# The end of a fill stage between attention and a feed-forward block: a second place for its x, earlier splits, stores reordered on the queue

## Chip, core, metric

One Trainium2 chip, one core. The metric is device time in microseconds (us) of one execution, from the first instruction to the last and the little around them. Engines: PE (TensorE: matmuls and their weight loads), DVE (VectorE), ACT (ScalarE), POOL (GpSimd), and SP, which here only issues transfers; ACT issues some too. Each engine works through its own list of instructions in order.

## The reference, cut

```
q_p, k_p = phi(q), phi(k)    # phi: x @ w_phi, minus max |.| of the row, then exp of it and of its negative
kv  = einsum('bhsf,bhsd->bhfd', k_p, v);  z = k_p.sum(axis=2)
num = einsum('bhsf,bhfd->bhsd', q_p, kv)
den = einsum('bhsf,bhf->bhs', q_p, z)[..., None] + 1e-06
x   = (num / den).transpose(0, 2, 1, 3).reshape(4608, 512)      # 8 batches of 576 tokens, 8 heads of 64
rms = sqrt(mean(x * x, axis=-1, keepdims=True) + 1e-06)
xn  = x / rms * rms_g
g, val = xn @ w_gate, xn @ w_val                                # 512 -> 1536
out = (g * sigmoid(g) * val) @ w_out                            # 1536 -> 512
```
All float32.

## The kernel before

**Attention.** 32 pairs (8 batches of 4 pairs of heads) run through a software pipeline: in loop turn i the front of pair i, the middle of pair i-1, the numerators of pair i-2 and the division of pair i-3 are interleaved. A matmul operand in float32 is written as a high part (a rounded copy, by ACT) and a low part (the difference), and a product is three matmuls: high by high, low by high, high by low. The helper `_split` (lines 60 and 61) makes such a pair.

**The division.** In `back`, a pair's denominators go to memory (`dd`, line 444), come back spread over partitions (`dr`, 448), are inverted on DVE (450), go out (`di`, 451) and come back broadcast (`rc`, 453; one buffer). `last` multiplies the numerators by them (467 and 468, DVE) and stores the result to `xs` (471 to 474, SP). These steps of one pair follow one another through memory.

**The fill.** The first three of the twelve 128-wide column blocks of both input weights (`fg`, `fv`) are ready during attention, and their products fill PE's gaps: 18 blocks of 256 tokens, b0 to b17. `fetch` (150, issued by ACT) loads a block's x, `fill` splits it (`xoh` by ACT, then `xol` by DVE), `squares` prepares the sum of squares (two ACT instructions, 157, and two POOL additions, 158 and 160), and six units follow, each of 12 matmuls (502): three column blocks by two weights. After two units one ACT copy (`fo`, 507) empties the PSUM bank, and a transfer that ACT issues stores it (508). `total` (165) sums the squares by four small matmuls, and a small ACT copy (`sums`, 167) takes the result. Some seven blocks are done with the last pairs; the rest follows in a loop at the end (699 to 716), together with the preparation of the remaining weights: `combine_u` (636) forms sums of quarters for a Strassen-like product in `stg` and splits them into `wh` and `wl` (DVE and POOL). `late()` puts instructions behind the last ones given to ACT, DVE and POOL so far.

**Places for x.** A block's x lies in the large buffer `xip` (even blocks) or in a side buffer (odd blocks). From loop turn 27 on the large one holds `x0`, the first 512 tokens for the next stage, and every block goes to the side buffer, one at a time: `load_x` then keeps one block in flight, and its transfer waits until the former block's `xol` has been read out of the buffer.

**Then** comes the feed-forward block over 9 blocks of 512 tokens (matmuls at line 772, evictions 780 to 800), and last the output product (line 1016). Both are untouched but for the buffer of `operands_x` (`sq`, `ss`). Tiles get their buffers from pools, and a scheduler with a cost model fixes the order in which each engine's list stands.

Of the kernel before, what the change touches and what calls it, by code (L numbers as in the profile page):

```python
# [82 lines left out]
def kernel(ctx: ExitStack, tc: tile.TileContext, q, k, v, w_phi,  # L83
# [60 lines left out]

    held = []

    def fetch(bk, n=T, queue=None):
        side = len(xips) > 1 and n == TF and (held or bk % 2)
        x = xips[-1 if side else 0].tile([128, NC * (TF if side else T)], F32, name="x")[:, 0:NC * n].rearrange("p (c t) -> p c t", c=NC)
        (queue or nc.sync).dma_start(out=x, in_=xsv[:, :, bk * n:(bk + 1) * n])  # L150
        return x

    def squares(x):
        ss = xm.tile([128, T], F32, name="ss", bufs=1)
        sq = xm.tile([128, T], F32, name="sq", bufs=1)
        for d, c in ((ss, 0), (sq, 2)):
            nc.scalar.activation(d.rearrange("p (c t) -> p c t", c=2), x[:, c:c + 2], AF.Square)
        nc.gpsimd.tensor_tensor(ss, ss, sq, ALU.add)
        s2 = xmf.tile([128, TF], F32, name="sl", bufs=2)
        nc.gpsimd.tensor_tensor(s2, ss[:, 0:TF], ss[:, TF:T], ALU.add)  # L160
        return s2
# [30 lines left out]

    waiting = set()

    @contextmanager
# [229 lines left out]
    def back(pr):  # L425
# [21 lines left out]
        def inv():  # L447
            nc.sync.dma_start(out=dr, in_=dd.rearrange("h (p x) -> (h p) x", p=64))
            with late():
                nc.vector.reciprocal(dr, dr)  # L450
            nc.sync.dma_start(out=di.rearrange("h (p x) -> (h p) x", p=64), in_=dr)
            rc = ndp.tile([64, 2, S], F32, name="rc", bufs=1)
            nc.sync.dma_start(out=rc, in_=di.unsqueeze(0).broadcast_to([64, 2, S]))
            d.update(nd=nd, rc=rc)

        return [(0.05, lambda: num(0, 0)), (0.2, lambda: num(0, 1)), (0.35, lambda: num(1, 0)),
                (0.5, lambda: num(1, 1)), (0.79, inv)]


    def last(pr):  # L460
        d = st.pop(pr)
        nd, rc, b, hp = d["nd"], d["rc"], d["b"], d["hp"]

        def fin():
            xt = nd[0]
            with late():
                nc.vector.tensor_tensor(xt[0:64], nd[0][0:64], rc[:, 0], ALU.mult)
                nc.vector.tensor_tensor(xt[64:128], nd[1][0:64], rc[:, 1], ALU.mult)
            r0, c0 = hp * 128, b * S
            if b % 2 == 0:  # L470
                nc.sync.dma_start(out=xs[r0:r0 + 128, c0:c0 + S], in_=xt)
            else:
                nc.sync.dma_start(out=xs[r0:r0 + 128, c0:c0 + SR], in_=xt[:, SM:S])
                nc.sync.dma_start(out=xs[r0:r0 + 128, c0 + SR:c0 + S], in_=xt[:, 0:SM])
            if hp == NP - 1:
                while blocks and blocks[0] * TF + TF <= (b + 1) * S:
                    fills.append(blocks.pop(0))

        return [(0.65 if pr < PR - 3 else 1.2, fin)]
# [5 lines left out]
    def fill(bk, xr):  # L485
        xx = dict(zip("hl", (xfp.tile([128, NC, TF], F32R, name="xo" + n) for n in "hl")))
        with late():
            _split(nc, xx["h"], xx["l"], xr)
        with late():
            s2 = squares(xr)  # L490
        o = {}

        def unit(j, wi):
# [11 lines left out]
            if wi:  # L505
                r = xfp.tile([128, 2, TF], F32, name="fo", bufs=3)
                nc.scalar.copy(r, fp)  # L507
                (nc.scalar if tail else nc.sync).dma_start(out=gvv[j][:, :, bk * TF:(bk + 1) * TF], in_=r)
# [20 lines left out]
    def load_x():  # L529
        while fills and len(here) < (1 if held else 2):  # L530
            bk = fills.pop(0)
            here.append((bk, fetch(bk, TF, nc.scalar)))

# [14 lines left out]
    for i in range(PR + 3):  # L548
# [20 lines left out]
        if i <= PR and len(units) + (len(fills) + len(here)) * J1 * 2 > RES:  # L569
# [4 lines left out]
            _merge([now])  # L574
        if i == PR - 5:
            x0 = fetch(0)
            held.append(x0)
        if not PR - 5 <= i < PR - 3:
            load_x()
        if i + 2 < PR:  # L580
# [55 lines left out]
    def combine_u(u):  # L636
# [7 lines left out]
        ve(t[:, 3], a12, t[:, 1], ALU.subtract)  # L644
        for src, o0, o1, eng in ((w[:, 0:2], OA11, OA22, nc.vector), (w[:, 3:4], OA22, OS1, nc.vector), (t, OS1, 7, nc.gpsimd)):
            for (hi, at_), (lo, _) in zip(places(u, o0, o1, 0), places(u, o0, o1, 1)):
                _split(nc, hi, lo, src[:, at_], lo_eng=eng)

    def operands_x(x, scratch=None):
# [4 lines left out]
        b11, b12, b21, b22 = X(0, 0), X(0, 1), X(1, 0), X(1, 1)  # L654
        t1, t2 = scratch or (xm.tile([128, T], F32, name=n, bufs=1).rearrange("p (c n) -> p c n", c=2) for n in ("sq", "ss"))
        po = nc.gpsimd.tensor_tensor
# [38 lines left out]
    with late():  # L695
        invert_new(1)
        ri = fetch_ri(0)
        norm(x0, ri)
    while units or here or fills:
        if len(units) <= 6:  # L700
            landed()
        now, units[:] = units[:6], units[6:]
        _merge([now])
        load_x()
        if len(preps) > 3:
            preps.pop(0)()
        left_ = len(units) + J1 * 2 * (len(here) + len(fills))
        if todo is None and left_ <= 18:
            with late():
                xb, todo = operands_x(x0, [stg[1][:, i * T:(i + 1) * T].rearrange("p (c n) -> p c n", c=2) for i in range(2)])  # L710
        with late():
# [377 lines left out]
```

## Time and profile before

| | |
|---|---|
| device time, 3 runs | 1277.21, 1280.15, 1286.79 us; median 1280.15 |
| the profiled execution | 1281.23 us, its span 1279.4 us |
| busy PE / DVE / ACT / POOL | 1231.3 / 958.4 / 743.1 / 701.3 us |
| mean granted clock of PE | 0.995 |
| attention, fill's end, feed-forward, output | to 488, 488 to 602, to 1014, to the end (us of the span) |

The profiled execution is 1.08 us above the median, and 1.83 us of it lie outside the span. Granted clock 1.00 is 2.4 GHz, and a window of 5 us with 0.66 holds some time at the other level, 1.2 GHz.

### The profile page before, as it was taken

What the parts mean: (1) busy time and instruction counts of PE and PEld (TensorE: products, weight loads), DVE (VectorE), ACT (ScalarE), POOL (GpSimd) and SP (SyncE); (2) the same over time, 40 slices, a digit from 0 to 9 for tenths busy, and PEclk for the clock granted to TensorE, in tenths of its full rate; (3) what the DMA queues carried; (4) which work ended last, traced back from release to release, by engine and by line L of the source; (5) the groups of instructions that cost most, each with busy time, mean ns of one, the idle gap of its engine ahead of it and who ended that gap; (6) DMA issues with size and microseconds to landing.
All of it is one profiled execution on the core that took longest, in us unless ns stands there. A gap on an engine that the chain in (4) does not pass through costs nothing. (4 is left out here: it accounts for less than half of the span.)

```text
span 1279.4 us, 27397 instructions
## 1 busy us (share of the span) xinstructions
PE 1231.3 (96%) x10401; PEld 1214.1 (95%) x10401; DVE 958.4 (75%) x1405; ACT 743.1 (58%) x1541; POOL 701.3 (55%) x649
## 2 busy tenths in 40 slices
PE   7989999999999999899999999999999899999998
PEld 7989999999999998899999999999999799999998
DVE  6998988988788653553758877877776788777785
ACT  6987897878778784564544445444434533344342
POOL 4766664667566553347435345543422067787776
PEclk9999999999999999999999999999999999999999
DMA  5555666666566425564445545556665643554443
GB/s 162 134 145 140 170 166 178 166 185 162 169 168 178 116 71 171 182 191 155 154 154 177 188 142 198 178 173 212 228 204 172 231 144 117 153 166 132 132 149 100
DMA packets 196977, 208.37 MB, mean 163 GB/s; under 512 B 67722, under 2 KB 148270, under 8 KB 196846
## 3 DMA queue, kind: packets, MB, share of 16 engines
q1 hardware_dynamic: 175982, 186.17, 48.2%
q10 hardware_dynamic: 20864, 20.45, 5.2%
q8 instruction: 82, 1.34, 0.4%
q14 instruction: 49, 0.40, 0.1%
HBM read 133.91 MB, written 72.67 MB: 161 GB/s over the span
## 5 line engine op out<-in xcount | busy, mean ns | idle before, releaser
L772 PE MATMUL r<-xo,wh 128*128 128x256 f32 x1764 | 309.9, 279 | 3.2 <-ACT c L783 1.4
L772 PEld LDWEIGHTS r<-xo,wh 128*128 128x128 f32 x1764 | 266.5, 188 | 4.7 <-ACT c L783 1.6
L405 POOL TENSOR_TENSOR ql<-eq,qh 128x256 fp32r<-128x256 f32 x256 | 215.5, 872 | 62.3 <-ACT qh L401 39.8
L772 PE MATMUL r<-xo,wl 128*128 128x256 f32 x882 | 240.9, 279 | 0.0
L772 PEld LDWEIGHTS r<-xo,wl 128*128 128x128 f32 x882 | 164.5, 188 | 0.0
L340 DVE TENSOR_REDUCE mx<-pp 128x4 f32<-128x512 f32 (+1 forms) x160 | 100.1, 631 | 48.4 <-PE pp L338 47.2
L376 PE MATMUL acc<-vm,ek 128*128 128x65 f32 x1024 | 129.9, 269 | 0.0
L376 PEld LDWEIGHTS acc<-vm,ek 128*128 128x128 f32 x1024 | 126.4, 192 | 0.1
L401 ACT ACTIVATE qh<-sm 128x512 fp32r<-128x512 f32 (+1 forms) x192 | 97.5, 508 | 0.0
L400 ACT ACTIVATE eq<-sm 128x512 f32<-128x512 f32 x128 | 78.7, 615 | 22.3 <-PE sm L389 20.7
L336 PE MATMUL pp<-wh,th 128*128 128x256 f32 x288 | 88.1, 307 | 2.7 <-DVE yk L343 1.2
L338 PE MATMUL pp<-wh,tl 128*128 128x256 f32 x288 | 84.5, 299 | 0.3 <-DVE tl L61 0.3
L502 PE MATMUL fp<-xoh,fg 128*128 128x256 f32 x344 | 73.9, 293 | 8.1 <-ACT fo L507 6.0
L337 PE MATMUL pp<-wl,th 128*128 128x256 f32 x288 | 81.7, 285 | 0.0
L61 POOL TENSOR_TENSOR xo<-x,xo 128x512 fp32r<-128x512 f32 x45 | 63.2, 1409 | 29.4 <-ACT xo L60 29.3
L363 ACT ACTIVATE ek<-yk 128x512 f32<-128x512 f32 x128 | 75.5, 656 | 2.9 <-DVE yk L343 2.6
L793 ACT ACTIVATE c<-c 128x1024 f32<-128x1024 f32 (+1 forms) x45 | 43.9, 976 | 52.6 <-DVE c L792 52.6
L502 PE MATMUL fp<-xoh,fv 128*128 128x256 f32 x344 | 72.1, 287 | 0.0
L407 POOL TENSOR_TENSOR ql<-eqr,qh 128x256 fp32r<-128x256 f32 x32 | 24.5, 765 | 84.6 <-ACT qh L401 84.6
L61 POOL TENSOR_TENSOR s2l<-st,s2h 128x768 fp32r<-128x768 f32 x17 | 39.8, 2340 | 56.1 <-ACT s2h L60 48.4
L54 POOL TENSOR_TENSOR stg<-stg,stg 128x128 f32<-128x128 f32 x48 | 24.5, 533 | 79.5 <-ACT c L789 36.4
L502 PEld LDWEIGHTS fp<-xoh,fg 128*128 128x128 f32 x344 | 57.9, 195 | 9.1 <-ACT fo L507 8.1
(263 smaller groups left out, 4166.6 us busy)
## 6 DMA issues: line engine op xcount, KB each, us to landing
ht<-hs SPq DMA_DIRECT2D x17, 1536.0 KB
hs<-c SPq DMA_DIRECT2D x36, 512.0 KB
gvr<-gvs SPq DMA_DIRECT2D x27, 512.0 KB
rc<-di SPq DMA_DIRECT2D x32, 288.0 KB
x<-xs ACTq DMA_DIRECT2D x18, 512.0 KB
x<-xs SPq DMA_DIRECT2D x9, 1024.0 KB
gvs<-fo ACTq DMA_DIRECT2D x35, 256.0 KB
kt<-in_k_dram SPq DMA_DIRECT2D x32, 256.0 KB
```

The costliest lines, as they stand in the source:

```text
L61: (lo_eng or nc.vector).tensor_tensor(lo, x, hi.bitcast(F32), ALU.subtract)
L336: nc.tensor.matmul(o, th[:, cs], wh, start=True, stop=False)
L337: nc.tensor.matmul(o, th[:, cs], wl, start=False, stop=False)
L338: nc.tensor.matmul(o, tl[:, cs], wh, start=False, stop=True)
L340: nc.vector.tensor_reduce(mx[:, 0:2 * m], pp[:, 0:2 * m], axis=AX.X, op=ALU.max, apply_absolute_value=True)
L363: nc.scalar.activation(e[h][:, sg], y["k", h], AF.Exp, scale=1.0 - 2.0 * sg)
L376: nc.tensor.matmul(acc[:, sg, h], e[h][:, sg, j], vm[:, h, j], start=False, stop=(h == 1 and j == T0 - 1))
L400: nc.scalar.activation(ei[:, sg], yi, AF.Exp, scale=1.0 - 2.0 * sg)
L401: nc.scalar.activation(hi[:, sg], yi, AF.Exp, scale=1.0 - 2.0 * sg)
L405: nc.gpsimd.tensor_tensor(lo[:, sg, cs], ei[:, sg, cs], hi[:, sg, cs].bitcast(F32), ALU.subtract)
L502: nc.tensor.matmul(fp[:, wi], w, xx[x][:, c], start=(wi == 0 and i == 0), stop=(i == 3 * NC - 1), skip_group_check=True)
L772: nc.tensor.matmul(self.r[r][:, k], w[:, cs], x[:, h, c], start=(first and k == 0 and i == 0), stop=(i == 3 * NP1 - 1), skip_group_check=True)
```

## The change

Seven edits. `fetch` gives an even block that finds the large buffer taken a second place, the tile `xo6` of the feed-forward stage's operands (empty until then). `x0` is loaded after the last block in the large buffer has been read, and multiplied by the norm (`norm`) with its operands. `load_x` keeps two blocks in flight. The loop at the end splits a block after the units of the one two places ahead, and the squares are one ACT instruction of 1024 columns behind ACT's latest. The middle eviction of a block is DVE's after attention. The lower parts of `t` in `combine_u` go from POOL to DVE. The stores of the last four pairs stand behind the latest `rc` load.

```
+            x = spare[0].tile([128, 2, 2, TF], F32R, name="xo6").bitcast(F32).rearrange("p a b t -> p (a b) t")
-        for d, c in ((ss, 0), (sq, 2)):
-            nc.scalar.activation(d.rearrange("p (c t) -> p c t", c=2), x[:, c:c + 2], AF.Square)
+        nc.scalar.activation(sq.rearrange("p (c t) -> p c t", c=NC), x, AF.Square)
...
+            loaded.append(latest(mybir.EngineType.SP))
...
+            with tc.issue_after(loaded[-1]) if pr >= PR - NP else nullcontext():
...
-        with late():
+        with tc.issue_after(latest(mybir.EngineType.Activation)):
             s2 = squares(xr)
...
-                nc.scalar.copy(r, fp)
+                (nc.vector.tensor_copy if ended and j == 1 else nc.scalar.copy)(r, fp)
...
-        while fills and len(here) < (1 if held else 2):
+        while fills and len(here) < 2:
...
-        if i == PR - 5:
-            x0 = fetch(0)
-            held.append(x0)
-        if not PR - 5 <= i < PR - 3:
-            load_x()
+        load_x()
...
-        for src, o0, o1, eng in ((w[:, 0:2], OA11, OA22, nc.vector), (w[:, 3:4], OA22, OS1, nc.vector), (t, OS1, 7, nc.gpsimd)):
+        for src, o0, o1, eng in ((w[:, 0:2], OA11, OA22, nc.vector), (w[:, 3:4], OA22, OS1, nc.vector), (t, OS1, 7, nc.vector)):
...
-        norm(x0, ri)
+    x0, held = None, [bk for bk, _ in here if bk % 2 == 0]
+    spare.append(xops[0])
+    if len(units) <= 6:
+        landed()
     while units or here or fills:
-        if len(units) <= 6:
-            landed()
+        if x0 is None and not any(bk in held for bk, _ in here):
+            x0 = fetch(0)
         now, units[:] = units[:6], units[6:]
         _merge([now])
+        landed()
         load_x()
...
             with late():
+                norm(x0, ri)
                 xb, todo = operands_x(x0, [stg[1][:, i * T:(i + 1) * T].rearrange("p (c n) -> p c n", c=2) for i in range(2)])
```

The order of the other instructions shifts as well, from about the first fill block on (the first difference on ACT is its squares, at 93 us of the span before), since the scheduler places them anew. The counts of PE's and SP's instructions stay the same; DVE has 20 more, POOL 11 and ACT 27 fewer.

SP's queue, at the denominators of the last two pairs, from the `rc` load of the last but one; before:

```order
L453 DMA rc<-di 64x1152
L444 DMA dd<-nd 1x576
L473 DMA xs<-nd 128x64
L474 DMA xs<-nd 128x512
L633 DMA stg_8088<-wgvs 128x1024
L444 DMA dd<-nd 1x576
L633 DMA wx<-wgvs 128x1024
L448 DMA dr<-dd 128x9
L451 DMA di<-dr 128x9
L453 DMA rc<-di 64x1152
```

and after:

```order
L458 DMA rc<-di 64x1152
L482 DMA xs<-nd 128x64
L483 DMA xs<-nd 128x512
L449 DMA dd<-nd 1x576
L639 DMA stg_8068<-wgvs 128x1024
L639 DMA wx<-wgvs 128x1024
L449 DMA dd<-nd 1x576
L453 DMA dr<-dd 128x9
L456 DMA di<-dr 128x9
L458 DMA rc<-di 64x1152
L482 DMA xs<-nd 128x64
L483 DMA xs<-nd 128x512
```

What moved are the stores of the last but one pair, which stood ahead of the last pair's second `dd` and now stand behind its `rc` (the stores at the top of the second list are those of the pair before it), and the weight load into `wx`, now ahead of that `dd`.

ACT's list for one block in the loop at the end (`L150`/`L153` is the load of a later block's x); before:

```order
L507 COPY fo<-fp 128x512
L167 COPY sums<-sm 128x2
L508 DMA gvs<-fo 128x2x256
L150 DMA x<-xs 128x4x256
L60 CAST wh_8072<-wx 128x512
L60 CAST wh_8072<-wx 128x256
L60 CAST wh_8072<-stg_8089 128x1024
L507 COPY fo<-fp 128x512
L157 ACTIVATE ss<-x 128x512
L157 ACTIVATE sq<-x 128x512
L508 DMA gvs<-fo 128x2x256
L507 COPY fo<-sm 128x512
```

and after:

```order
L516 COPY fo<-fp 128x512
L169 COPY sums<-sm 128x2
L60 CAST xoh<-xo_8196 128x1024
L158 ACTIVATE sq<-xo_8196 128x1024
L517 DMA gvs<-fo 128x2x256
L153 DMA xo_8308<-xs 128x4x256
L60 CAST wh_8052<-wx 128x512
L60 CAST wh_8052<-wx 128x256
L60 CAST wh_8052<-stg_8069 128x1024
L517 DMA gvs<-fo 128x2x256
L516 COPY fo<-sm 128x512
```

The split and the squares of a block now stand right behind an eviction and ahead of the next load; before, the load stood between them, and the `fo` copy that is missing now is DVE's.

DVE's list at the start of the feed-forward block (`L747`/`L761` and later evict it; `fg`, `wx` belong to the last weights); before:

```order
L641 TENSOR_TENSOR stg_8089<-stg_8088 128x256
L642 TENSOR_TENSOR stg_8089<-stg_8088 128x256
L61 TENSOR_TENSOR fg_86<-stg_8088,fg_85 128x512
L61 TENSOR_TENSOR fg_86<-stg_8088,fg_85 128x256
L747 TENSOR_TENSOR gvr<-gvr,ri 128x1024
L800 TENSOR_TENSOR c_9116<-c_9116,c_9117 128x2x256
L643 TENSOR_TENSOR stg_8089<-stg_8089,stg_8088 128x256
L749 TENSOR_TENSOR gvr<-gvr 128x512
L799 TENSOR_TENSOR c_9116<-c_9116,r_9118 128x2x256
L644 TENSOR_TENSOR stg_8089<-stg_8088,stg_8089 128x256
```

and after:

```order
L61 TENSOR_TENSOR fg_86<-stg_8068,fg_85 128x512
L61 TENSOR_TENSOR fg_86<-stg_8068,fg_85 128x256
L761 TENSOR_TENSOR gvr<-gvr,ri 128x1024
L814 TENSOR_TENSOR c_9080<-c_9080,c_9081 128x2x256
L649 TENSOR_TENSOR stg_8069<-stg_8069,stg_8068 128x256
L763 TENSOR_TENSOR gvr<-gvr 128x512
L813 TENSOR_TENSOR c_9080<-c_9080,r_9082 128x2x256
L650 TENSOR_TENSOR stg_8069<-stg_8068,stg_8069 128x256
L806 TENSOR_TENSOR c_9187<-c_9187,r_9203 128x2x256
L61 TENSOR_TENSOR fg_86<-stg_8069,fg_85 128x768
L810 TENSOR_TENSOR c_9188<-c_9188,r_9189 128x512
L61 TENSOR_TENSOR wx<-stg_8069,wx 128x256
```

The lower parts of 128x768 (`fg`) and 128x256 (`wx`) are new here, and once more for `fv`; they were POOL's.

## Rows read from the trace of the kernel before

**Rows 1.** Windows by stage: from:to, length, busy us of each engine, granted clock, DMA, GB/s.
```profile
107.00:480.00 373.00, 364.75 (x3071) 358.88 (x3071) 302.45 (x525) 302.53 (x737) 230.35 (x288) 1.00 0.57 155
487.84:601.90 114.06, 104.82 (x866) 103.00 (x865) 51.52 (x63) 56.41 (x104) 53.53 (x39) 0.97 0.57 176
487.84:521.00 33.16, 27.30 (x216) 26.65 (x215) 8.22 (x12) 10.70 (x21) 5.61 (x6) 0.95 0.59 182
521.00:601.90 80.90, 77.53 (x653) 76.35 (x652) 43.30 (x52) 45.70 (x84) 47.92 (x33) 0.98 0.56 173
615.00:642.00 27.00, 25.59 (x217) 25.19 (x217) 26.29 (x36) 12.78 (x22) 15.09 (x9) 1.00 0.44 149
```

**Rows 2.** The same columns for the fill's matmuls (line 502) alone.
```profile
487.84:601.90 114.06, 101.13 (x816) 98.03 (x816) 0.97 0.57 176
515.00:520.00 5.00, 4.33 (x25) 4.03 (x24) 0.66 0.59 203
566.00:571.00 5.00, 4.18 (x22) 4.18 (x23) 0.66 0.54 192
```

**Rows 3.** Timeline: start, length, engine, line, tiles; PE from 531.64 to 537.45.
```profile
531.64 0.28 PE L502 MATMUL sm<-xoh,fg 128*128 128x256 f32 x1
...
534.36 0.28 PE L502 MATMUL fp<-xoh,fg 128*128 128x256 f32 x1
...
536.97 0.28 PE L502 MATMUL fp<-xoh,fv 128*128 128x256 f32 x1
...
537.45 0.36 PE L502 MATMUL fp<-xoh,fg 128*128 128x256 f32 x1
```

**Rows 4.** Waits of PE from 487.84 to 604: us, times, longest.
```profile
PE fp L502 <- ACT fo L507: 6.0, 3, 3.5
PE fp L502 <- ACT sums L167: 1.8, 3, 0.8
```

**Rows 5.** Timeline of ACT and its queue; in brackets idle before, and its releaser.
```profile
513.65 0.37 ACTq L150 DMA_DIRECT2D x<-xs  x1
514.11 0.59 ACT L507 COPY fo<-fp 128x512 f32<-128x512 f32 x1 [6.54 <-DVE xol L61]
...
533.08 0.93 ACT L60 CAST wh<-wx 128x512 fp32r<-128x512 f32 x2 [3.16 <-DVE xol L61]
```

**Rows 6.** Timeline of DVE, 493 to 538.
```profile
493.42 1.41 DVE L467 TENSOR_TENSOR nd<-nd,rc 64x576 f32<-64x576 f32 x1 [7.03 <-DMA rc<-di]
...
505.10 0.21 DVE L450 RECIPROCAL dr<-dr 128x9 f32<-128x9 f32 x1 [2.50 <-DMA dr<-dd]
...
510.79 0.75 DVE L467 TENSOR_TENSOR nd<-nd,rc 64x576 f32<-64x576 f32 x1 [5.20 <-DMA rc<-di]
...
512.33 1.23 DVE L61 TENSOR_TENSOR xol<-x,xoh 128x1024 fp32r<-128x1024 f32 x1
...
533.07 4.92 DVE L187 SCALAR_TENSOR_TENSOR x<-x,g,ri 128x512 f32<-128x512 f32 x4 [0.43 <-DMA ri<-rid]
```

**Rows 7.** Timeline of SP's queue, 496 to 507: when each transfer is issued.
```profile
496.06 0.32 SPq L473 DMA_DIRECT2D xs<-nd  x1
...
496.91 0.42 SPq L633 DMA_DIRECT2D stg<-wgvs  x1
497.43 0.26 SPq L444 DMA_DIRECT2D dd<-nd  x1
...
507.07 0.46 SPq L453 DMA_DIRECT2D rc<-di  x1
```

**Rows 8.** Groups of 487 to 604: busy us, mean ns | idle before, releaser.
```profile
L61 POOL TENSOR_TENSOR wl<-stg,wh 128x1024 fp32r<-128x1024 f32 x6 | 14.3, 2390 | 24.8 <-ACT wh L60 24.8
...
L61 DVE TENSOR_TENSOR xol<-x,xoh 128x1024 fp32r<-128x1024 f32 x10 | 14.0, 1402 | 12.3 <-ACT xoh L60 12.2
```

**Rows 9.** Waits of PE from 600 to 700.
```profile
PE r L772 <- DVE c L799: 1.4, 2, 1.2
```

**Rows 10.** A window inside the attention stage; columns as in the first group.
```profile
280.00:285.00 5.00, 4.44 (x24) 4.44 (x25) 1.77 (x4) 1.60 (x5) 2.93 (x4) 0.66 0.90 270
```

More of the change, by code (lines that the diff above doesn't have):

```diff
@@ L1 @@
-from contextlib import ExitStack, contextmanager
+from contextlib import ExitStack, contextmanager, nullcontext
 import concourse.bass as bass
@@ L143 @@
     sums = gl.tile([128, N // 128], F32, name="sums")
-    held = []
+    spare = []
     def fetch(bk, n=T, queue=None):
-        side = len(xips) > 1 and n == TF and (held or bk % 2)
-        x = xips[-1 if side else 0].tile([128, NC * (TF if side else T)], F32, name="x")[:, 0:NC * n].rearrange("p (c t) -> p c t", c=NC)
+        if n == TF and spare and bk % 2 == 0:
+            x = spare[0].tile([128, 2, 2, TF], F32R, name="xo6").bitcast(F32).rearrange("p a b t -> p (a b) t")
+        else:
+            side = n == TF and bk % 2
+            x = xips[-1 if side else 0].tile([128, NC * (TF if side else T)], F32, name="x")[:, 0:NC * n].rearrange("p (c t) -> p c t", c=NC)
         (queue or nc.sync).dma_start(out=x, in_=xsv[:, :, bk * n:(bk + 1) * n])
@@ L153, in squares @@
     def squares(x):
-        ss = xm.tile([128, T], F32, name="ss", bufs=1)
-        sq = xm.tile([128, T], F32, name="sq", bufs=1)
-        for d, c in ((ss, 0), (sq, 2)):
-            nc.scalar.activation(d.rearrange("p (c t) -> p c t", c=2), x[:, c:c + 2], AF.Square)
-        nc.gpsimd.tensor_tensor(ss, ss, sq, ALU.add)
+        sq = xm.tile([128, 2 * T], F32, name="sq", bufs=1)
+        nc.scalar.activation(sq.rearrange("p (c t) -> p c t", c=NC), x, AF.Square)
+        ss = sq[:, 0:T]
+        nc.gpsimd.tensor_tensor(ss, ss, sq[:, T:2 * T], ALU.add)
         s2 = xmf.tile([128, TF], F32, name="sl", bufs=2)
@@ L193, with latest @@
     waiting = set()
+    def latest(eng):
+        return next(i for i in reversed(nc.cur_bb.bb.instructions[-300:]) if i.engine == eng)
     @contextmanager
@@ L454, in inv @@
             d.update(nd=nd, rc=rc)
+            loaded.append(latest(mybir.EngineType.SP))
         return [(0.05, lambda: num(0, 0)), (0.2, lambda: num(0, 1)), (0.35, lambda: num(1, 0)),
                 (0.5, lambda: num(1, 1)), (0.79, inv)]
+    loaded = []
     def last(pr):
@@ L469, in fin @@
             r0, c0 = hp * 128, b * S
[L470 to L474, printed above, removed]
+            with tc.issue_after(loaded[-1]) if pr >= PR - NP else nullcontext():
+                if b % 2 == 0:
+                    nc.sync.dma_start(out=xs[r0:r0 + 128, c0:c0 + S], in_=xt)
+                else:
+                    nc.sync.dma_start(out=xs[r0:r0 + 128, c0:c0 + SR], in_=xt[:, SM:S])
+                    nc.sync.dma_start(out=xs[r0:r0 + 128, c0 + SR:c0 + S], in_=xt[:, 0:SM])
             if hp == NP - 1:
@@ L529, in load_x @@
     def load_x():
-        while fills and len(here) < (1 if held else 2):
+        while fills and len(here) < 2:
             bk = fills.pop(0)
-            here.append((bk, fetch(bk, TF, nc.scalar)))
+            with tc.issue_after(latest(mybir.EngineType.Activation)) if tail else nullcontext():
+                here.append((bk, fetch(bk, TF, nc.scalar)))
     def landed():
@@ L654, in operands_x @@
         b11, b12, b21, b22 = X(0, 0), X(0, 1), X(1, 0), X(1, 1)
-        t1, t2 = scratch or (xm.tile([128, T], F32, name=n, bufs=1).rearrange("p (c n) -> p c n", c=2) for n in ("sq", "ss"))
+        if not scratch:
+            sq = xm.tile([128, 2 * T], F32, name="sq", bufs=1)
+            scratch = [sq[:, i * T:(i + 1) * T].rearrange("p (c n) -> p c n", c=2) for i in range(2)]
+        t1, t2 = scratch
         po = nc.gpsimd.tensor_tensor
```

## The prediction

> **What bounds the kernel now.** I read the windows by stage first. Over the whole run TensorE is busy 1231.3 of 1279.4 us, so only its idle time and its time at the lower clock can be won. Most of what this change touches lies between the last numerators (487.84) and the first matmul of the feed-forward block (601.90): 114.06 us, of which PE is busy 104.82, so idle 9.24, at a mean granted clock of 0.97 [rows 1]. The split at 521.00 shows where: 5.86 of the idle time is in the first 33.16 us, 3.37 in the other 80.90 [rows 1].
>
> Then the fill's matmuls alone. The stage holds 816 of them [rows 2]: 24 left over and 11 blocks of 72. When nothing disturbs them, 24 take from 531.64 to 534.36, 0.1133 us each; where the sums stand between two of them, the step is 0.48 (536.97 to 537.45), 0.37 more [rows 3]. So the stage can't be shorter than 816 x 0.1133 + 11 x 0.37 = 92.5 + 4.1 = 96.6 us, and its **excess is 17.5 us**. Of that, 9.24 is idle. Two windows of 5 us show clock 0.66, that is, time at 1.2 GHz right behind idle stretches: 25 and 22 matmuls in 4.33 and 4.18 us of busy time [rows 2], which at 0.1133 would take 2.83 and 2.49, so 1.5 and 1.7 us are lost to the clock. Idle time and clock together make 12.4 us: 7.4 in the first part and 5.1 in the second. The other 5.1 no row of mine names.
>
> Next the waits: PE's largest in the stage is for the PSUM bank that ACT's `fo` copy must empty, 6.0 us in three waits, the longest 3.5; ACT's `sums` copy adds 1.8 [rows 4]. Last, what ACT did then. At 513.65 its queue issues the load of the next block's x, and the `fo` copy behind it starts at 514.11 after 6.54 us idle, released by DVE's `xol` [rows 5]: the load may not start before `xol` has read the one place, and the copy stands behind the load in ACT's list. That `xol` ran at 512.33, behind the multiplications of the last pair, which began at 510.79 after 5.20 us of waiting for `rc` [rows 6]. And `rc` was late because SP's queue held the last pair's second `dd` until 497.43, behind the stores of pair 30 (496.06), which wait for multiplications that themselves began at 493.42 after a wait of 7.03 for their own `rc` [rows 6, 7]. In the later blocks the same pattern is smaller: at 533.08 ACT starts a copy after 3.16 us, released by `xol` [rows 5].
>
> **The change part by part.** *Stores behind `rc`.* The last `dd` no longer waits for multiplications of pair 30. From `dd` to `rc` took 497.43 to 510.79, 13.4 us [rows 6, 7]; issued at about 490, after the numerators end at 487.84 and are evicted, it lets the last multiplications start near 503, some 7 us earlier. What is queued behind the moved stores: the loads of the last blocks' x, which need the last pair's rows in memory. They wait for the last multiplications anyway, and these come earlier; I cost the move at nothing there. The chain has a new neighbour: `stg` and `wx`, the weight loads, now stand ahead of that `dd` on SP. Each issue takes about 0.4 us [rows 7], so 0.8 us if they can start at once.
>
> *Two places, split two blocks ahead.* The load of a later block then waits for an `xol` that lies a block back, and stands behind a split that is done early. The 6.0 us of `fo` waits lose their cause. What is late next is the `xol` of the second block, behind the last multiplications on DVE: 503 + 1.5 + 1.23 = 505.7 [rows 6]. The block in work at that time began at about 497.3, when its `xol` ended (493.42 + 1.41 + 1.2 + 1.23) [rows 6], and lasts 72 x 0.1133 + 0.37 = 8.5, until 505.8. So it is just in time; I leave 1.4 of the first part's 7.4 us, and **gain 6**. In the second part ACT has a copy and an instruction of squares fewer in each block, and its load waits for nothing that is late; I leave 1.1 of 5.1 and **gain 4**. Of the 5.1 us without a name I take **2**, since what follows an idle stretch goes with it. Together 12; the bounds are 0 (every wait finds a successor) and 17.5 (the whole excess).
>
> *Copies and lower parts to DVE.* In the stage, DVE is busy 43.30 of 80.90 us in the second part [rows 1]. POOL's lower parts of 128x1024 took 2390 ns each, six of them; on DVE the nearest row is `xol` of the same shape, 1402 ns [rows 8]: six cost 8.4 us there. Nine `fo` copies of 512 columns at the 0.59 of ACT [rows 5] are 5.3 more: 57 of 81, hidden beside PE as long as the order doesn't put a copy behind a wait. Taken at zero here; if that cover is gone it is the rival below. The multiplication of `x0` by the norm, 4.92 us in four instructions at 533 [rows 6], now comes some four blocks later, ahead of the operands of the first feed-forward group. By the order those are the last work of the stage on POOL and DVE, so the bounds are 0 and 3 us (most of the multiplication), and I take **1**, nearer to zero since the block it falls in has slack of about 2.5 (8.5 less 57/81 of it).
>
> *The start of the feed-forward block.* From 615 to 642 DVE is busy 26.29 of 27.00 us, PE 25.59 [rows 1], and PE already waits there for DVE (line 799): 1.4 us [rows 9]. The change adds lower parts of 128x768 and 128x256, twice: 2 x 1024 columns at 1.23 to 1.40 per 1024 [rows 6, 8], 2.5 to 2.8 us. Bounds 0 and 2.8; POOL, which shares these tiles, does less, and PE has 1.4 us idle to begin with. I take **1**.
>
> *Squares in one instruction, and the new order in attention.* The squares cost ACT less by one instruction a block; ACT isn't the bound (56.41 of 114.06 [rows 1]). The scheduler's new order from 93 us on has no row of its own. PE idles 8.25 us from 107 to 480 [rows 1], and a window such as 280 to 285 has 24 matmuls at clock 0.66 [rows 10], where 5 / 0.1133 = 44 would fit: 20 x 0.1133 = 2.3 us per such event beside its idle time. One event more or less is the bound, about 2.3 + 3.5 (the longest wait in [rows 4]), so 5.8 both ways; I take **0**.
>
> Sum: 12 - 1 - 1 = 10 us gained, 1281.2 - 10 = 1271.2. The profiled execution lies 1.1 above the median of 1280.15, and three runs spread over 9.6 us, so I make no further correction and round to **1271.5**.
>
> A rule of the Trainium skill speaks against the first term. "DMA: Bandwidth & Descriptors", section "Issuing engines are not separate DMA queues", says that transfers from any issuing engine run on the same 16 DMA engines and interleave. By it the weight loads ahead of `dd` slow the small transfers behind them, and the first part's gain would go: the second rival, where the time is worked out without it. The trace is undecided: the second `dd` of the last pair, issued beside `stg` and `wx`, needed until 505.10 for the reciprocal, 7.7 us for two small steps [rows 6, 7], and no row shows it without them.
>
> **The rivals.** *All of it comes back* (0.16): PE runs without a gap, and nothing is lost later: 1281.2 - 17.5 = 1263.7. For it: every wait in the first part hangs on one chain. Against: 5.1 us without a name, and DVE's full load at 615.
>
> *The chain stays as late* (0.13): `dd` leaves earlier, but behind the weight loads, whose tiles must be free; SP waits there as it did for the stores, or the transfers take longer together. Then the last multiplications stay near 510.8, and the `xol` of the second block, behind them on DVE, comes at 513.6, 7.8 us after PE wants it. The first part gains nothing: 1281.2 - 4 - 2 + 2 = 1277.2.
>
> *DVE takes ACT's place* (0.09): a `fo` copy stands behind lower parts that wait for ACT's `wh`. On POOL these waits were 24.8 us in six [rows 8], 4.1 each. If PE sees an eighth of that, 0.5 us, in seven blocks, the second part's 4 and the unnamed 2 are gone and 3.5 come on top: 1281.2 - 6 + 3.5 + 2 = 1280.7.
>
> *Attention loses* (0.06), slower than before: the new order there leaves PE idle for as long as the longest wait of today, 3.5 us [rows 4], and each is followed by a stretch at 1.2 GHz: 5.8 us each. Two such events cancel the gain; three give 1271.2 + 17.4 = 1288.6. For it: the order differs from 93 us on, in nearly four fifths of that stage. Against: PE is busy 364.75 of 373.00 there [rows 1], and the instructions are the same.
>
> **How the numbers follow.** The forecast has 0.56 and spreads over about 1266 to 1277. One per cent, 12.8 us, is about what a measurement of this kernel can tell from no change; faster by more means below 1267.3, slower means above 1293. Below lie nearly all of the first rival (0.15) and a sixth of the forecast (0.09): 0.24. Above lies only the far end of the last rival with four events: 0.03. The rest is 0.73. The range is 1264 to 1281: it leaves out half of the first rival, half of the third and the last, 0.08 + 0.05 + 0.06.
>
> **What would show it.** In the changed kernel's profile the stage from the last numerators to the first feed-forward matmul should be near 102 us, clock 0.98 or more, with no `fo` wait above 1.5 us. The last `rc` multiplications should start 14 to 16 us after the numerators end (now 23). At the start of the feed-forward block PE's waits for DVE's line 799 (then 813) should grow to 2 or 3 us. I would be wrong if PE's busy time outside this stage moves by more than 3 us, if SP's queue holds `dd` behind `stg`, or if waits for DVE's `fo` appear.

## The result and the profile after

| | before | after |
|---|---|---|
| median, 4 runs each | 1280.74 us (1277.21 to 1286.79) | 1267.54 us (1263.76 to 1273.57) |
| ratio, 95% interval | | 0.9886 [0.9845, 0.9928] |
| profiled execution, span | 1281.23, 1279.4 us | 1266.87, 1265.1 us |
| PE busy | 1231.3 us | 1221.9 us |

The change makes the kernel 1.1% faster, 13.2 us in the medians; the forecast was 1271.5. Later runs, beside the experiments, gave 0.9933 (e5_after_again, below). The intervals overlap between 0.990 and 0.993, so a gain of 0.7 to 1.0%, 9 to 13 us, agrees with both.

The windows of the changed kernel, with the columns of [rows 1]. The last matmul of the numerators ends at 490.15, and most of the stage lies between there and 596.00. For the kernel before, the 487.84 of [rows 1] is where that matmul starts; it ends 0.29 us later, at 488.13, and the comparisons below go by the ends:

```profile
487.84 0.29 PE L440 MATMUL sm<-qh,kv1l 128*65 128x288 f32 x1
```

The changed kernel:

```profile
490.15:596.00 105.85, 102.14 (x875) 101.28 (x874) 57.80 (x83) 53.26 (x89) 42.26 (x33) 1.00 0.63 205
490.15:515.00 24.85, 22.18 (x188) 21.73 (x187) 6.64 (x7) 9.70 (x17) 6.40 (x6) 1.00 0.73 247
...
523.00:596.00 73.00, 71.96 (x619) 71.55 (x620) 47.50 (x68) 40.30 (x68) 33.74 (x25) 1.00 0.61 192
605.00:632.00 27.00, 25.53 (x223) 25.24 (x221) 26.92 (x40) 12.63 (x22) 8.57 (x6) 1.00 0.47 157
```

Where the stage of before ran at a mean clock of 0.97, all of these windows show 1.00: the two stretches at 0.66 of [rows 2] have no counterpart, and neither have the idle stretches ahead of them. PE is idle for 3.7 of 105.85 us (9.2 of 114.06 before), and 2.7 of these lie in the first 25 us. The start of the feed-forward block (last line) has DVE busy 26.92 of 27 us.

PE's waits from 484 to 600, which answer to [rows 4]:

```profile
PE fp L511 <- DVE xol L61: 1.5, 1, 1.5
PE fp L511 <- ACT sums L169: 1.2, 3, 0.5
PE r L786 <- DVE io L179: 0.9, 1, 0.9
```

No wait for the `fo` copy is left. What took its place is a wait for `xol`, 1.5 us. DVE's timeline shows where that comes from (compare [rows 6]):

```profile
507.74 0.75 DVE L475 TENSOR_TENSOR nd<-nd,rc 64x576 f32<-64x576 f32 x1 [6.76 <-DMA rc<-di]
...
509.30 1.22 DVE L61 TENSOR_TENSOR xol<-x,xoh 128x1024 fp32r<-128x1024 f32 x1
```

The last multiplications begin at 507.74, 17.6 us behind the end of the numerators (510.79 - 488.13 = 22.7 before), and the `xol` stands behind them. On ACT's queue, the next load of x still waits for that `xol`, and the `fo` copy behind it is held 4.1 us, but PE doesn't need it at once (compare [rows 5]):

```profile
510.56 0.37 ACTq L153 DMA_DIRECT2D x<-xs  x1
511.02 0.59 ACT L516 COPY fo<-fp 128x512 f32<-128x512 f32 x1 [4.11 <-DVE xol L61]
```

On SP's queue (compare [rows 7]) the second `dd` is out at 492.89, 2.7 us after the numerators, with both weight loads ahead of it:

```profile
490.62 0.32 SPq L639 DMA_DIRECT2D stg<-wgvs  x1
492.28 0.32 SPq L639 DMA_DIRECT2D wx<-wgvs  x1
492.89 0.23 SPq L449 DMA_DIRECT2D dd<-nd  x1
498.04 0.32 SPq L453 DMA_DIRECT2D dr<-dd  x1
...
503.19 0.45 SPq L458 DMA_DIRECT2D rc<-di  x1
503.69 0.58 SPq L482 DMA_DIRECT2D xs<-nd  x1
```

The queue isn't free of waits either. Ahead of `wx` it stands for 1.3 us, by the profile for the `rc` load of the pair before, and the second `dd` stands behind it:

```profile
SPq L639 <- DMA rc<-di: 1.3, 1, 1.3
```

PE's waits from 596 to 700, at the start of the feed-forward block (compare [rows 9]):

```profile
PE r L786 <- DVE fv L61: 1.5, 1, 1.5
PE r L786 <- DVE c L800: 0.6, 1, 0.6
PE r L786 <- DVE c L813: 0.3, 1, 0.3
```

A wait of 1.5 us for the low part `fv`, which POOL used to make, is new; the wait for line 813 (799 before) fell from 1.4 to 0.3 us.

### The profile page after: what moved, and what is told of

The parts are those of the page before. It is cut to its first block, busy times and chain, and to the rows that moved or that the text cites. A ratio compares the mean times of both kernels' runs of the same rounds, so it can differ in the third digit from the quotient of the medians.

```text
span 1265.1 us, 27382 instructions
## 1 busy us (share of the span) xinstructions
PE 1221.9 (97%) x10401; PEld 1206.2 (95%) x10401; DVE 963.8 (76%) x1425; ACT 738.1 (58%) x1514; POOL 684.5 (54%) x638
## 4 chain that ended last, share of the span: by engine, by line
PE 69%; DVE 15%; DMA 5%; ACT 4%; issue 4%; POOL 1%; ACTq 0%; SPq 0%; DVEq 0%; POOLq 0%
PE r L786 20%; PE fp L511 8%; PE gz L1030 6%; PE gd L1030 5%; PE gy L1030 5%; PE acc L381 5%; PE sm L445 3%; PE fp L1030 3%; PE sm L511 2%; PE pp L341 2%; PE pp L343 2%; PE pp L342 2%; PE sm L328 2%; PE fp L445 2%; PE sm L394 2%
## 5 line engine op out<-in xcount | busy, mean ns | idle before, releaser
L54 POOL TENSOR_TENSOR wa<-raw,wa 128x192 f32<-128x192 f32 x64 | 41.7, 672 | 43.8 <-DVE wa L52 18.2
## 6 DMA issues: line engine op xcount, KB each, us to landing
rc<-di SPq DMA_DIRECT2D x32, 288.0 KB
```

## How the runs are compared by stage

Device times of one kernel spread over some 10 to 20 us, more than most edits are worth. The profiles tell them apart better, since in the two kernels that were profiled twice most of the spread lies in other stages. For each profile the **stage** is the time from the end of the last numerators to the end of ACT's first feed-forward eviction, plus 0.1133 us for each fill matmul beyond 480 that ran ahead of the numerators' end (482 recorded before, 506 in every kernel with the single square). For the changed kernel: 596.96 - 490.15 + 26 x 0.1133 = 109.8; for the kernel before: 606.90 - 488.13 + 2 x 0.1133 = 119.0. "Start" is the time from there to the fortieth of the copies by which ACT evicts the feed-forward block. All times are in us.

| kernel | stores | places | moves | stage | start | ratio of times [95%] |
|---|---|---|---|---|---|---|
| before, two profiles | - | - | - | 119.0, 120.4 | 113.3, 114.2 | 1 |
| e6_stores_only | yes | - | - | 116.1 | 112.8 | 0.9953 [0.9924, 0.9981] |
| e9_moves_only | - | - | yes | 116.1 | 112.7 | 0.9963 [0.9946, 0.9980] |
| e7_places_only | - | yes | - | 120.6 | 114.9 | 0.9993 [0.9958, 1.0028] |
| e1_no_stores | - | yes | yes | 117.9 | 114.6 | 0.9976 [0.9958, 0.9993] |
| e2_dve_back | yes | yes | - | 114.5 | 114.9 | 0.9935 [0.9912, 0.9957] |
| e3_one_place | yes | - | yes | 111.2 | 112.7 | 0.9921 [0.9896, 0.9947] |
| after, two profiles | yes | yes | yes | 109.8, 109.5 | 112.3, 112.4 | 0.9886 and 0.9933 |

"Places" stands for the second place, the splits two blocks ahead and the late load of `x0`; "moves" for the eviction and the lower parts on DVE. Two profiles of one kernel differ by 0.2 to 1.4 us in the stage. All variants were profiled once, so a difference of 1 to 1.5 us between two rows is not shown. The runs e1 to e4, e5 to e8 and e9 to e12 stood on three chips, where the kernel before has medians of 1278.44, 1282.54 and 1276.72; times are compared by their ratios, and the expectations that are given in us (from 1267.5) can be read against the measured us only roughly. By the ratios alone the changed kernel, e2 and e3 can't be told apart: their intervals overlap.

A longer start alone is not a loss. From there to ACT's last such copy the kernels differ the other way: 287.7 us in the changed kernel, 284.6 in e11 with a start of 115.5, 285.6 in e7 with 114.9.

## Experiments

**The changed kernel again (e5_after_again).**

> The changed kernel as it is, on the chip of the runs beside it. If its gain is a property of the kernel: 0.986 to 0.991 of the time before. Where that lies against the variants without the stores (0.9976), without the moves to DVE (0.9935) and with one place (0.9921) says what each edit is worth.

Measured: 1273.01 us (12 runs) against 1282.54 (34 runs), ratio 0.9933 [0.9898, 0.9968]; stage 109.5, start 112.4. The stage repeats within 0.3 us; the ratio doesn't: 0.9933 lies outside the 0.986 to 0.991 that were expected, though its interval reaches into them.

**Stores back (e1_no_stores).**

```
-            with tc.issue_after(loaded[-1]) if pr >= PR - NP else nullcontext():
+            with nullcontext():
```

> The changed kernel with the stores of the last pairs back in their old place on SP's queue. If the chain of the last denominators bounds the first part of the stage (the prediction's first term), the last multiplications come 3 to 6 us later, PE waits for the split behind them, and part of the time at 1.2 GHz returns: 1270 to 1273 us. If the second place and the early splits hide that chain by themselves: within 1 us of the changed kernel's 1267.5.

Measured: 1275.13 us, ratio 0.9976, stage 117.9, so 8.2 us of the stage's gain is gone. PE's wait for `xol`, and DVE's last multiplications:

```profile
PE fp L511 <- DVE xol L61: 6.9, 1, 6.9
```

```profile
510.76 0.75 DVE L475 TENSOR_TENSOR nd<-nd,rc 64x576 f32<-64x576 f32 x1 [5.96 <-DMA rc<-di]
```

The multiplications begin 23.5 us behind the numerators' end (487.24) again, 6 us later than in the changed kernel, and PE waits 5.4 us longer for the split behind them; then the window from 510 to 515 has clock 0.62. The first theory holds: the second place does not hide the chain of the last denominators.

**Places alone (e7_places_only).** The changed kernel without stores and moves:

```
-            with tc.issue_after(loaded[-1]) if pr >= PR - NP else nullcontext():
+            with nullcontext():
...
-                (nc.vector.tensor_copy if ended and j == 1 else nc.scalar.copy)(r, fp)
+                nc.scalar.copy(r, fp)
...
-        for src, o0, o1, eng in ((w[:, 0:2], OA11, OA22, nc.vector), (w[:, 3:4], OA22, OS1, nc.vector), (t, OS1, 7, nc.vector)):
+        for src, o0, o1, eng in ((w[:, 0:2], OA11, OA22, nc.vector), (w[:, 3:4], OA22, OS1, nc.vector), (t, OS1, 7, nc.gpsimd)):
```

> The changed kernel without the edit of the stores and without the moves to DVE: second place, splits two blocks ahead, late load of the first 512 tokens and the single square are left. If the second place carries the gain by itself: 0.990 to 0.993 of before. If it waits for the last multiplications all the same: PE waits 5 us or more for the split behind them, and the time is 0.996 to 1.002 of before.

Measured: 1283.24 us, ratio 0.9993, stage 120.6. PE waits for `xol`:

```profile
PE fp L511 <- DVE xol L61: 9.1, 2, 6.8
```

The second theory holds: the waits for the copy became a wait of 6.8 us for the split.

**Stores alone (e6_stores_only).** Against the kernel before:

```
+            loaded.append(next(i for i in reversed(nc.cur_bb.bb.instructions[-300:]) if i.engine == mybir.EngineType.SP))
...
+            with tc.issue_after(loaded[-1]) if pr >= PR - NP else nullcontext():
```

> The kernel before with the stores of the last pairs behind the latest rc load and nothing else. If the late chain of the last denominators was what cost the first part of the stage: the last multiplications begin 3 to 5 us earlier, the wait of 3.5 us for the fo copy goes, and the time is 0.993 to 0.996 of before. If the stores pay only together with the second place: within 0.2% of before.

Measured: 1275.96 us, ratio 0.9953, stage 116.1, 3.6 us less than the mean of the two profiles before. The last multiplications begin 19.7 us behind the numerators' end (485.26), 3 us earlier than before:

```profile
504.96 1.51 DVE L470 TENSOR_TENSOR nd<-nd,rc 64x576 f32<-64x576 f32 x1 [8.37 <-DMA rc<-di]
```

The waits became smaller and did not go:

```profile
PE fp L506 <- ACT fo L511: 3.8, 2, 2.0
PE fp L506 <- ACT sums L167: 2.7, 3, 2.0
PE sm L506 <- DVE xol L61: 1.4, 1, 1.4
```

So the stores pay alone, but less than with the rest: with one place, the load of the next block and the copy behind it still wait for each `xol`.

**One place (e3_one_place).** The places of x, the loop at the end and the load of `x0` as before; the rest changed.

```
-        while fills and len(here) < 2:
+        while fills and len(here) < (1 if spare else 2):
...
+        if i == PR - 5:
+            x0 = fetch(0)
+            spare.append(x0)
...
-        landed()
         load_x()
...
```

> The changed kernel with one place for the fill's x from turn 27 on, a block's load in flight at a time, splits where they were, and the first 512 tokens loaded and multiplied early as before; the stores, the single square, the copies and lower parts on DVE stay changed. If the second place and the early splits carry the gain: the waits for the fo copy come back, with two of the stretches at 1.2 GHz, and the time is 1275 to 1279 us. If the stores and the moves to DVE carry it: 1270 or less.

Measured: 1269.79 us, ratio 0.9921, stage 111.2. The rival holds: without the second place and the early splits only 1.5 us of the stage is lost, about what two profiles of one kernel can differ by. No wait for a `fo` copy is back. PE's largest wait in it is another one, for `sums`, and one window behind it (495 to 500) has clock 0.70:

```profile
PE fp L509 <- ACT sums L167: 3.9, 3, 3.2
```

**Both moves back (e2_dve_back).** The last two pairs of lines of e7_places_only, and not the first.

> The changed kernel with the middle eviction back on ACT and the lower parts of t back on POOL. If these moves only fill idle time (the prediction's zero), the time stays within 1.5 us of 1267.5, and at the start of the feed-forward block the waits for DVE fall by 1 to 2 us. If ACT's list was what PE waited for, the second part of the stage loses 3 us or more: 1271 or above.

Measured: 1271.04 us, ratio 0.9935, stage 114.5, start 114.9: 4.9 and 2.5 us more than changed. By the stage the rival holds; by the time nothing is told, since the changed kernel's second ratio is 0.9933. The start did not get shorter without the moves but longer, and about 1 of the 2.5 us comes back behind it (286.7 us to the last copy, 287.7 in the changed kernel). Which of the two moves is it?

**Eviction on ACT (e10_fo_on_act)**, lower parts on DVE.

```
-                (nc.vector.tensor_copy if ended and j == 1 else nc.scalar.copy)(r, fp)
+                nc.scalar.copy(r, fp)
```

> The changed kernel with all three evictions of a block on ACT; the lower parts of t stay on DVE. With both moves back the stage took 114.5 us instead of 109.7. If the eviction is what ACT lacked time for: about 114. If it was POOL's lower parts: about 110.

Measured: 1272.76 us, ratio 0.9974 [0.9953, 0.9995], stage 115.3, start 115.8. PE's list has no wait for a `fo` copy, so ACT's time for the copies isn't what shows. DVE's timeline and PE's waits:

```profile
522.65 3.77 DVE L189 SCALAR_TENSOR_TENSOR x<-x,g,ri 128x512 f32<-128x512 f32 x4 [6.86 <-DMA ri<-rid]
526.34 1.21 DVE L61 TENSOR_TENSOR xol<-x,xoh 128x1024 fp32r<-128x1024 f32 x1
```

```profile
PE fp L511 <- DVE xol L61: 4.4, 2, 2.4
...
PE sm L177 <- DVE sums L175: 1.2, 1, 1.2
```

The scheduler, with other work on DVE, put the multiplication of `x0` by the norm (line 189) ahead of an `xol`; it waited 6.86 us for `ri` and held that split, and PE waited 2.4 us for it, at 527.6. (The other wait for `xol`, 2.0 us at 506.9, is the one behind the last multiplications, 1.5 in the changed kernel.) In the changed kernel the same multiplication starts at 561.76, behind a split. The order goes with the eviction: counted from 480 us, the multiplication stands behind the fourth split in the three variants that have the two places and the middle eviction on ACT (e2, e7, e10), and behind the ninth in the others with two places. In e2, where PE waits 2.4 us as well:

```profile
526.54 3.62 DVE L189 SCALAR_TENSOR_TENSOR x<-x,g,ri 128x512 f32<-128x512 f32 x4 [7.01 <-DMA ri<-rid]
```

So 2.4 us of this loss come from the order on DVE. Some 3 more come at the end of the stage, where PE waits 1.2 us for `sums` and the next window has clock 0.66: 29 matmuls in 4.97 us, where 29 x 0.1133 = 3.3 would do.

```profile
595.00:600.00 5.00, 4.97 (x29) 4.97 (x30) 2.22 (x3) 1.22 (x3) 0.00 (x0) 0.66 0.86 268
```

Why the end comes out so in this variant was not looked into.

**Lower parts on POOL (e11_wl_on_pool)**, middle eviction on DVE: the last pair of lines of e7_places_only alone.

> The changed kernel with the lower parts of t back on POOL; the middle eviction stays on DVE. If POOL's 2.4 us each held up the weights and the operands of the first group: the stage takes about 114 us instead of 109.7, and the feed-forward start about 2 us more. If not: about 110.

Measured: 1272.69 us, ratio 0.9960 [0.9939, 0.9981], stage 113.8, start 115.5. The order on DVE stays as in the changed kernel here; the durations don't. DVE's multiplication by the norm and the next `xol`, then POOL at that time:

```profile
561.19 5.41 DVE L189 SCALAR_TENSOR_TENSOR x<-x,g,ri 128x512 f32<-128x512 f32 x4
...
568.91 2.30 DVE L61 TENSOR_TENSOR xol<-xo,xoh 128x1024 fp32r<-128x1024 f32 x1
```

```profile
562.98 2.40 POOL L61 TENSOR_TENSOR wl<-stg,wh 128x1024 fp32r<-128x1024 f32 x1 [0.42 <-ACT wh L60]
568.65 1.49 POOL L160 TENSOR_TENSOR sq<-sq 128x512 f32<-128x512 f32 x1 [3.27 <-ACT sq L158]
```

The same two in the changed kernel:

```profile
561.76 3.26 DVE L189 SCALAR_TENSOR_TENSOR x<-x,g,ri 128x512 f32<-128x512 f32 x4
...
568.59 1.22 DVE L61 TENSOR_TENSOR xol<-xo,xoh 128x1024 fp32r<-128x1024 f32 x1
```

Four instructions take 5.41 us instead of 3.26, while POOL works on its own lower part (2.40 us). The split takes 2.30 instead of 1.22, beside an addition of squares on POOL that here begins 0.26 us ahead of it, and in the changed kernel 0.63 us behind its start (at 569.22). PE then waits 1.8 us for that split, and the next window is at clock 0.67:

```profile
570.00:575.00 5.00, 3.73 (x19) 3.73 (x20) 4.00 (x5) 1.56 (x3) 4.92 (x4) 0.67 0.24 88
```

The Trainium skill, "SBUF — State Buffer", section "Who interferes with whom", says that a DVE instruction with two inputs in SBUF contends with a GpSimd instruction that reads SBUF. The trace agrees: the 2.15 us more are nearly the 2.40 of POOL's instruction.

**Moves alone (e9_moves_only).** Against the kernel before, with the lower parts of `t` on DVE as well:

```
-                nc.scalar.copy(r, fp)
+                (nc.vector.tensor_copy if ended and j == 1 else nc.scalar.copy)(r, fp)
```

> The kernel before with the middle eviction of the end's blocks on DVE and the lower parts of t on DVE, and nothing else. If the moves are worth something by themselves, the stage from the last numerators to the first feed-forward eviction is 2 to 4 us shorter than the 119 us of before (2.7 was the difference of the variants without the stores). If they pay only when the stores are moved: within 1 us of 119, or longer, because the copies on DVE wait behind the last multiplications.

Measured: 1273.21 us, ratio 0.9963, stage 116.1, start 112.7. The moves are worth some 3.6 us of the stage by themselves (2.9 and 4.3 against the two profiles before). PE's waits for the `fo` copy, to be compared with [rows 4]:

```profile
PE fp L502 <- ACT fo L507: 4.4, 2, 3.6
```

The wait behind the last multiplications is as long as before (3.6 us); the later one, 1.9 and 1.7 us near 566.8 in the two profiles before, is gone.

**Weight loads behind the last chain (e4_weights_last).**

```
...
+    for w in (stg[0], wx.bitcast(F32).rearrange("p o n -> p (o n)")):
+        nc.sync.dma_start(out=w[0:1, 0:S], in_=lastdi[0][0:1, 0:S])
     fetch_u(0)
     fetch_u(1)
```

> The changed kernel with the first two weight loads (stg, wx, 1 MB) held behind the last pair's rc load by two small transfers of 2.3 KB each that are written to the same tiles first; nothing else moves on any engine. If transfers of all queues slow each other, dd to rc falls from 14.9 us to about the 10.1 us of the pair before, the last multiplications begin near 503 instead of 507.7, and PE's 2.7 us of idle time in 490 to 515 falls to about 1: 1265 to 1266. If the weight loads cost that chain nothing: dd to rc stays at 14 to 15, and the time within 0.7 us of 1267.5.

Measured: 1271.99 us, ratio 0.9945 [0.9925, 0.9966], stage 113.7. SP's queue and the last multiplications:

```profile
490.03 1.49 SPq L449 DMA_DIRECT2D dd<-nd  x2
496.20 0.34 SPq L453 DMA_DIRECT2D dr<-dd  x1
```

```profile
505.46 0.75 DVE L476 TENSOR_TENSOR nd<-nd,rc 64x576 f32<-64x576 f32 x1 [7.45 <-DMA xs<-nd]
```

Counted from the end of the last `dd` issue (491.52) to the multiplications (505.46) the chain took 13.9 us; in the changed kernel, with 1 MB of weights just ahead, 492.89 + 0.23 to 507.74, 14.6. From `dd` to the issue of `dr` it was 4.7 and 4.9. So from the issue of `dd` on the weight loads cost that chain some 0.7 us, not the 4 to 5 of the first theory. Ahead of it they cost more: counted from the numerators' end the multiplications come at 15.6 us (505.46 - 489.82) and not at 17.6. The other 1.3 us is the wait of SP ahead of `wx`, which here no longer stands ahead of the second `dd`. The release of the multiplications is now, by the profile, a store of the pair before (`xs`), which the edit of the stores had put behind `rc`, so `rc` itself may have been there a little earlier. The time of this run tells less, since the edit added a wait of its own: a `fo` copy was held until the small transfer into `wx` had landed.

```profile
505.87 0.58 ACT L517 COPY fo<-fp 128x512 f32<-128x512 f32 x1 [5.65 <-DMA wx<-di]
```

**Splits ahead of the last multiplications (e8_split_first).**

```
...
-            with late():
+            with tc.issue_after(end_[0]) if end_ else late():
                 nc.vector.tensor_tensor(xt[0:64], nd[0][0:64], rc[:, 0], ALU.mult)
...
-        if 0 <= i - 3 < PR:
+        if 0 <= i - 3 < PR - 1:
...
+        if i == PR + 2:
+            if len(units) <= 6:
+                landed()
+            end_.append(latest(mybir.EngineType.DVE))
+            _merge([last(PR - 1)])
```

> The changed kernel with the last pair's multiplications put behind the splits of the two blocks that follow on DVE (they stood ahead of them). If what is left of the stall is that order: PE's wait of 1.5 us for the split and ACT's wait of 4.1 us go, and the time is 1 to 3 us below the changed kernel's on the same chip. If the later end of the last pair then delays the loads of the last two blocks: PE waits for their x near 560 to 580, and nothing is gained.

Measured: 1268.76 us, ratio 0.9895 [0.9860, 0.9930] against 0.9933 for the changed kernel beside it; stage 108.4, the shortest of all. DVE's timeline:

```profile
512.26 1.23 DVE L61 TENSOR_TENSOR xol<-x,xoh 128x1024 fp32r<-128x1024 f32 x1 [7.90 <-ACT xoh L60]
513.40 1.85 DVE L475 TENSOR_TENSOR nd<-nd,rc 64x576 f32<-64x576 f32 x1
```

The last multiplications now begin at 513.40, later than in any kernel here, and PE has no wait for `xol` left. So nothing in the stage needs that pair early; what cost time was that a split stood behind it. Whether this beats the changed kernel can't be told from the times, whose intervals overlap.

**The kernel before, again (e12_before_again).**

> The kernel before, profiled a second time. What of the 14.4 us between the two profiles lies in one execution only shows here: if the late part of the gain (3.3 us behind the first feed-forward groups) is the kernel's, it is there again; if it belongs to that execution, the stages behind the first groups take 287 to 288 us as in the variants, and the stage before them again about 119.

Measured: 1279.12 us; stage 120.4, start 114.2, and from there to the last eviction 288.0 us, where the first profile had 291.0 and the changed kernel 287.7. So 3 us of the 14.4 between the first two profiles belong to one execution, the first of the kernel before. What is left by stages, from the means of two profiles each: 119.7 - 109.65 = 10.0 in the stage and 113.75 - 112.35 = 1.4 at the start, together 11.4 us.

## Why the prediction was right, and where it was not

**The total.** Forecast 10 us, 11.4 by the stages and 9 to 13 by the times: right, and partly by luck. The stage gave 1 us less than the 11 net, the start of the feed-forward block 1.4 more where 1 less was forecast, and inside the stage a gain booked under the places belongs to the stores and to moves that had been taken at zero.

**Stage.** Forecast 12 gross, less 1 for late operands; 10.0 came. Clock 1.00 and no `fo` wait above 1.5 us came as said. The prediction's own measure (102 us to the first feed-forward matmul) needs a correction, since the changed kernel runs 11 of these matmuls in gaps of the fill. The first one behind the fill:

```profile
591.68 0.28 PE L786 MATMUL r<-xo,wl 128*128 128x256 f32 x1
```

591.68 - 490.15 - 11 x 0.1133 + 26 x 0.1133 gives 103.2, against 601.87 - 488.13 + 2 x 0.1133 = 114.0 before: close to the forecast. Up to the first eviction less is left, 9.2 us between the first two profiles, since PE then idles again, 0.9 us of it for `io`.

**Stores behind `rc`, 7 us earlier, and "two places, gain 6".** The chain of waits was read rightly, but the gain was booked under the places, while the working needed the stores for it. The places alone gain nothing (120.6), and without them 1.5 us is lost, hardly more than two profiles differ by; the stores gain 3.6 alone and 8.2 with the rest. The last multiplications came 5.1 us earlier against the numerators, at 17.6 us and not at 14 to 16. Of the miss 0.8 us is the later issue of `dd`, 2.7 us behind the numerators and not 1.9 (490 - 488.13), with the wait of 1.3 us for `wx` ahead of it, where 0.8 was costed for two issues that start at once. Another 1.5 us is the chain: 14.9 us from 492.89 to 507.74, where 13.4 was carried over from the kernel before (the rest is the rounding of 503.4 to 503). The sign "if SP's queue holds `dd` behind `stg`" came in part. In the second part of the stage "its load waits for nothing that is late" was right.

**The chain stays as late** (second rival) was half right: the chain got 1.5 us longer, but it started earlier. Of the two mechanisms that it named, the wait of SP with the weight loads was there, at 1.3 us and not at the length of the stores' wait. The other, slower transfers, explains little of the longer chain: from the end of the issue of `dd` to the issue of `dr` it took 3.4 us before and 4.9 after, and 4.7 with the weight loads out of the way (e4). Of the Trainium skill's rule ("DMA: Bandwidth & Descriptors", section "Issuing engines are not separate DMA queues") that transfers interleave, this run shows 0.7 us in the chain.

**Copies and lower parts to DVE, taken at zero**: the step that failed. By the stage of one profile each they are worth 3.6 us alone and 4.9 in company; the ratio of e9, 0.9963 [0.9946, 0.9980], shows a gain alone, while that of e2 doesn't tell it from the changed kernel. Three causes were seen: a late wait for the `fo` copy that goes (e9), DVE's instructions beside POOL's that take longer (e11), and the scheduler's order on DVE, which puts the multiplication of `x0` where it holds a split or where it doesn't (e10, e2). How they share the 4.9 us is not shown.

**The start of the feed-forward block, a loss of 1**: a gain of 1.4 (113.75 to 112.35). DVE has more work there, as said, and one new wait of 1.5 us for its `fv`; the waits for line 813 fell to 0.3 us where 2 to 3 were forecast. The relief of POOL doesn't explain it: the start takes 112.8 with the lower parts on POOL in e6, and 114.6 with them on DVE in e1. The cause stays open.

**DVE takes ACT's place** (third rival) did not come. **Attention**: the end of the numerators, corrected for the fill in the same way, lies at 487.9 and 486.8 us in the two profiles before, at 487.2 and 491.4 in the two after, and from 483 to 488 in the others. The single square and the new order show no effect beyond that. PE's busy time outside the stage fell by 5.7 us between the first two profiles, at equal work (1231.3 - 109.5 before; 1221.9 - 103.1 - 24 x 0.1133 after), more than the 3 us that the prediction named as a sign of being wrong; but the second profile before has 1116.9 there against 1116.1 after, so this too belongs to one execution.

**Open:** why `dr` follows the issue of `dd` by 4.7 to 5.2 us for this pair in e4 and the changed kernel, by 3.4 in the kernel before (497.43 + 0.26 to 501.09), and by 2.3 for the pair before (482.18 + 0.31 to 484.77 in the changed kernel). The transfers of x and of the former pair run at the same time; taking those away was not tried.

## What to carry to other kernels

Before giving an operand a second buffer, look at what stands ahead of the instruction that makes it on its engine: here a split waited behind a division that nobody needed yet, and putting the division earlier cut that wait to 1.5 us, putting it behind the split removed it, while the buffer alone gained nothing. An instruction moved off an engine that is not the bound can still pay, because it had slowed a neighbour or because the scheduler's order falls otherwise; cost such moves from the order and from the neighbour's durations, not from busy shares. Where executions spread by 1%, compare stages of profiles with equal work before trusting medians.

## What was not expected of the hardware

In two of the fourteen profiled executions PE's matmuls come 4% slower in the whole last stage although the granted clock is 1.00. Two windows of 24 us in the output product, of the changed kernel and then of e8_split_first:

```profile
1045.00:1069.00 24.00, 24.00 (x214) 24.00 (x213) 18.24 (x15) 10.66 (x16) 20.33 (x10) 1.00 0.34 98
```

```profile
1042.70:1066.70 24.00, 24.00 (x207) 24.00 (x206) 17.96 (x16) 10.33 (x15) 20.31 (x10) 1.00 0.37 100
```

PE is busy throughout, with 214 matmuls in the one and 206 in the other. From ACT's last copy of the feed-forward block to the end the changed kernel took 268.1 and 268.0 us in its two profiles, this execution of e8 277.1 and that of e7 276.9, while their feed-forward stages ran at the usual pace. That is 9 us for which no edit touches the stage. Each of the two kernels was profiled once, so it isn't shown that another execution of them would run at the usual pace, nor how much of the spread of times this makes. What sets it stays open.
